# An mLSTM cell with mixture-of-depths: where gates, stores, weights and expert layers stand in a hand-ordered schedule

## The chip, the core and the metric

The kernel runs on one core of a Trainium2 chip. A core has TensorE (PE; its weight loads are shown as PEld), VectorE (DVE), ScalarE (ACT), GpSimd (POOL) and SyncE (SP), which take their instructions each from a queue of its own, in the order in which the program puts them there, and wait for one another at semaphores. SyncE issues nearly all transfers, which 16 DMA engines carry out; GpSimd issues the indirect ones. The metric is the time of one execution on the device in microseconds, lower is better. Beside it stands the span from the first to the last instruction, which the profile divides up.

## The reference

Four batches, eight heads, 768 positions, heads of 40. First a recurrent cell with a matrix state for each head, then a feed-forward network for the 128 rows of each batch that score highest:

```python
for t in range(S):
    m_new = np.maximum(f_gate[:, :, t] + m, i_gate[:, :, t])
    f_stab, i_stab = np.exp(f_gate[:, :, t] + m - m_new), np.exp(i_gate[:, :, t] - m_new)
    C = f_stab[..., None, None] * C + i_stab[..., None, None] * np.einsum('bhd,bhe->bhde', vt, kt)
    n = f_stab[:, :, None] * n + i_stab[:, :, None] * kt
    h_tilde = np.einsum('bhde,bhe->bhd', C, qt)
    denom = np.maximum(np.abs(np.einsum('bhd,bhd->bh', n, qt))[:, :, None], 1.0)
    y[:, :, t] = 1.0 / (1.0 + np.exp(-o_gate[:, :, t])) * h_tilde / denom
# x: y with the heads side by side, (4, 768, 320)
scores = np.einsum('bsd,d->bs', x, w_gate)
for b in range(B):
    top_idx = np.argpartition(-scores[b], capacity)[:capacity]       # capacity 128
    xe = x[b, top_idx]
    ye = np.maximum(xe @ w1, 0.0) @ w2                                # 320 -> 1024 -> 320
    out[b, top_idx] = xe + sigmoid(scores[b, top_idx])[:, None] * ye  # other rows: x
```

All is float32. The inputs and the output are in device memory.

## The kernel before

`_fast` computes the cell in chunks: 12 steps, n = 0 to 11, of 256 positions each, three to a batch (batch b = n // 3). All stabilising factors are worked out once at the start from the two gate arrays (`gate_rows`, `gate_cols`); the result is a column of factors for each step.

**One step.** TensorE runs `scores(n)` (k times q, line 307), then for the next step `turn(n+1, "kT")` (the transposes of k, line 241, with `fill` matmuls of line 230 ahead of them in some steps) and `update(n+1)` (v times k, line 274), then `read(n)` (state times q, 329), `turn(n+1, "qT")` and `attend(n)` (masked scores times v, 339). VectorE masks the scores (`masked`, 313), sums the states (`states`, 286 to 294) and divides (`divide`, 348 to 353) into a tile y. ScalarE copies the transposes out of PSUM (243, 245), widens q (225) and takes the sigmoid of the output gate (`sigmoid`, 257). GpSimd multiplies v by its factors two steps ahead (`weigh(n+2)`, 253) and y by the gate (`output`, 361, two instructions), which gives x, the rows of the bridge between both parts.

**Buffers.** k, q and v have three each, the gate o four, y four, x two (batches alternate). A load into a buffer waits for the last reader of what it held.

**Loads.** `load(n)` puts v, k (two transfers each) and q (one) of step n on SyncE, and in most steps the gate of step n-1 (four transfers). It is called three steps ahead. `store(n)` writes x of a step to the output in two transfers; `load` holds some of these, and others stand in the loop. The weights of the expert (eight transfers) are put on SyncE in step 5. SyncE also holds a transfer until the eighth before it has landed.

**The expert of a batch.** `router(n)` (376) takes a step's scores on VectorE. `spread(b)` (404, 408) brings the 768 scores of a batch into every partition, `ranks(b)` counts for each score how many are greater, three columns on VectorE (414) and three on ScalarE (419), `select(b)` (453) makes a one-hot tile `sel` of it, `numbers(b)` (498, 459 to 464) the row numbers, `fetch(b)` (504) brings these rows back out of the output by an indirect transfer on GpSimd; it waits for the batch's stores. `fetched(b)` (514 to 518) transposes them, `layer1` (543 to 549, two calls for two halves) and `layer2` (559) are the network, `weighed` (564) applies the gate of the expert, and `add(b)` (568) adds the result into the output by an indirect transfer. The last batch, 3, is done in another way: its rows are picked out of x by matmuls (`picked`, 479), and its scores are spread in two parts (`ranks_first`, `ranks_last`).

**Where the expert's parts stand before.** Batch 0: `spread` in step 3, `ranks` and `select` in step 5, `numbers` at the end of step 5, `fetch` at the end of step 6 ahead of which `weigh(8)` and behind which `weigh(9)` stands on GpSimd, layers in step 8. Batch 1: `spread` in step 6, `numbers` and `fetch` in step 8, `layer1` in step 9, `layer2` in step 10. Batch 2: `spread` in step 9, `ranks` in step 10 directly behind `layer2(1)`, `fetch` in step 10, the first half of `layer1` in step 11 and the second half behind the loop. TensorE's order in the loop is written out by hand; no scheduler moves anything. What follows the loop from `router_last` on is the end of batch 3 with `layer2(2)` in it.

Of the kernel before, what the change touches and what calls it, by code (L numbers as in the profile page):

```python
# [9 lines left out]
FP = mybir.dt.float32  # L10
# [16 lines left out]
def _fast(ctx, tc, q, k, v, i_gate, f_gate, o_gate, w_gate, w1_in, w2_in, out):  # L27
# [32 lines left out]
    def load_kv(n, t, src):  # L60
        b, s = divmod(n, NS)
        for c in range(2):
            a = s * 256 + c * 128
            SP.dma_start(out=t[n % NB][:, c, :, 0:D], in_=src[b, :, a:a + 128, :].rearrange("h p d -> p h d"))
# [12 lines left out]

    def load(n):

        if n < N:  # L80
            load_kv(n, v_t, v)
            load_kv(n, k_t, k)
            for i in {8: (2,), 9: (3, 4, 5)}.get(n, ()):
                store(i)
            load_q(n)
            for i in {7: (0, 1)}.get(n, ()):
                store(i)
        for i in {7: (), 8: (), 9: (6, 7, 8), 11: (), 12: (10, 11)}.get(n, (n - 1,) if n <= N else ()):
            load_o(i)

    for t, src in ((f_sb, f_gate), (i_sb, i_gate)):
# [21 lines left out]
    load_kv(2, v_t, v)  # L113
    load_kv(2, k_t, k)
    load_q(2)
    load_o(1)
    ident = const.tile([128, 128], FP, name="ident")

    def zero(t):
# [223 lines left out]
    def divide(n):  # L343
        b, s = divmod(n, NS)
        pH = pending[n]["pH"].rearrange("s h r x -> s r h x")
        den = work.tile([128, 2, H], FP, name="den")
        nq = pH[:, :, :, D]
        DVE.scalar_tensor_tensor(out=den, in0=nq, scalar=-1.0, in1=cols[s][:, 2:4, b * H:b * H + H], op0=OP.mult, op1=OP.max)
        DVE.scalar_tensor_tensor(out=den, in0=nq, scalar=LEAST * LEAST, in1=den, op0=OP.max, op1=OP.max)
        rec = work.tile([128, 2, H], FP, name="rec")  # L350
        DVE.reciprocal(out=rec, in_=den)
        y = work.tile([128, 2, H, D], FP, name="y", bufs=4)
        DVE.tensor_tensor(out=y, in0=pH[:, :, :, 0:D], in1=rec.unsqueeze(3).to_broadcast([128, 2, H, D]), op=OP.mult)
        pending[n]["y"] = y

# [231 lines left out]
    zero(wv_t[2].rearrange("s c h r x -> s c h (r x)"))  # L587
    zero(k_t[2][:, :, :, D:DP])
    weigh(1)
    for n in range(N):  # L590
        b, s = divmod(n, NS)
        more = n + 1 < N
        late = b > 1 and s == 1
        given = late or n == 5
        if n > 0:
            load(n + 3)
        if n == 5:
            for h in range(2):
                f, g = slice(512 * h, 512 * h + 512), slice(2 * h, 2 * h + 2)
                SP.dma_start(out=w1[:, :, f], in_=w1_in[0:256, f].rearrange("(j p) f -> p j f", j=2))  # L600
                for i in range(2):
                    SP.dma_start(out=w1c[64 * i:64 * i + 64, g],
                                 in_=w1_in[256:DM, :].rearrange("p (f i e) -> p i f e", i=2, e=128)[:, i, g])
            for h in range(2):
                SP.dma_start(out=w2[:, 4 * h:4 * h + 4], in_=w2_in[512 * h:512 * h + 512].rearrange("(f p) d -> p f d", p=128))
        for i in {10: (9,), 11: (10,)}.get(n, ()):
            store(i)
        scores(n)
        masked(n)
        if n == 8:  # L610
            fetched(0)
            numbers(1, ps_t.tile([128, 3], FP, name="pi", tag="t"))
            fetch(1)
        if n == 8:
            valued(0)
        if n == 0:
            update(0)
            load(3)
            states(0)
        if n == 8:  # L620
            layer1(0, 0)
            layer1(0, 4)
            layer2(0, 0, 4)
            layer2(0, 4)
        if n == 10:
            layer2(1)
        if given:
            ranks(b - 1)
            select(b - 1)
        if n in (8, 10):  # L630
            weighed(n // 2 - 4)
        if n == 9:
            fetched(1)
            sigmoid(8)
            output(8)
            for i in range(6, 9):
                store(i)
            weigh(10)
            layer1(1, 0)
            layer1(1, 4)  # L640
            valued(1)
            router(6)
            router(7)
        early = n in (3, 6) or n > 8
        if n > 0 and early:
            router(n - 1)
        if more:
            turn(n + 1, "kT", (0, 2, 2, 2, 2, 3, 4, 5)[n] if n < 8 else 0)
            widen(n + 1)
        if 0 < n and more:  # L650
            update(n + 1)
            states(n + 1)
        if 0 < n < 7 and not early:
            router(n - 1)
        if not more:
            sigmoid(n)
            gated(n)
            fill(ps_t.tile([128, 128], FP, name="pf", tag="t"), 2)
        read(n)
        if n == 10:  # L660
            numbers(b - 1, spare(n + 1)[:, 1, 0:3])
        if n + 2 < N and n != 8:
            weigh(n + 2)
        if n == 10:
            fetch(2)
        if n == 0:
            update(1)
            states(1)
        if more:
            turn(n + 1, "qT")  # L670
            if b > 0 and s == 0:
                dep[b - 1] = {"sb": spread(b - 1, 0, 2 * NS)}
            if n not in (6, 7, 8):
                sigmoid(n)
        else:
            fetched(b - 1, 2)
            dep[b] = {"sb4": spread(b, 0, 4)}
            layer1(b - 1, 0)
            valued(b - 1)
            ranks_first(b)  # L680
        attend(n)
        divide(n)
        if n == 5:
            numbers(b - 1, spare(n + 1)[:, 1, 0:3])
        if n == 8:
            for i in (6, 7):
                sigmoid(i)
                output(i)
        elif more and n not in (6, 7):
            output(n)  # L690
        if n == 6:
            fetch(0)
        if n in (8, 10):
            add(n // 2 - 4)
        if n == 0:
            tables()
        if n == 1:
            margins()
    b = B - 1
    router_last(N - 1)  # L700
    output(N - 1)
    layer1(b - 1, 4)
# [371 lines left out]
```

## Time and profile before

| | |
|---|---|
| median of 14 runs | 169.01 us (167.5 to 171.79) |
| the profiled execution | 168.81 us |
| its span | 167.1 us |
| PE busy | 147.9 us, 88% |
| PEld, DVE, ACT, POOL busy | 128.7, 94.7, 75.9, 68.9 us |
| DMA queue of SyncE and its packets | 93472, 22.36 MB, 71.7% of 16 engines' span |
| granted TensorE clock, mean | 0.978 |

The times of TensorE's parts, from its timeline: the scores of steps 1 to 11 start at 20.32, 28.35, 36.81, 45.57, 53.94, 62.72, 72.12, 81.15, 99.56, 118.40 and 130.22 us; the layers of batch 0 run from 82.24 to 92.91; `layer2(2)` starts at 141.66, the last matmul of `layer2(3)` ends at 159.95, and the rest of the span is the last indirect add.

In lines of a timeline the columns are start, length, engine, source line, operation, out<-in, shapes and count, and in brackets the idle time ahead of it and what ended it. In lines of waits they are engine and line, what it waited for, us in total, how often, and the longest. Packets of 160 bytes (k, v and o, whose rows are 40 floats) make up 73728 of the trace's 94438, with a mean of 16.3 ns each.

### The profile page before, as it was taken

The numbers are of one execution on the slowest core, as the hardware profiler recorded it, in microseconds if no ns is written. First come the engines' busy times: TensorE is split into PE (matmuls) and PEld (weight loads), VectorE is DVE, ScalarE is ACT, GpSimd is POOL, SyncE is SP. The second block draws the span as 40 slices with busy tenths as digits, with TensorE's granted clock in tenths as the row PEclk, the third lists the DMA queues.
The fourth block names the chain that finished last, engine by engine and source line by source line (L and its number), as shares of the span: only waits on it lengthen the run. The fifth ranks groups of instructions, "written<-read, shape, count | busy, mean of one in ns | idle before, by whom it ended". The sixth has DMA issues, their size and how long they took to land.

```text
span 167.1 us, 6707 instructions
## 1 busy us (share of the span) xinstructions
PE 147.9 (88%) x2872; PEld 128.7 (77%) x2872; DVE 94.7 (57%) x250; ACT 75.9 (45%) x144; POOL 68.9 (41%) x89
## 2 busy tenths in 40 slices
PE   7999989799989797997999996949999999999920
PEld 7888879697969696996897785739869989799710
DVE  6576456476655999869620049633695796802000
ACT  1576564443626952494421353441935339521110
POOL 7045293909082907262006128953410682230030
PEclk9999999999999999999999999986999999999995
DMA  4999989898899979789968988999687160330003
GB/s 88 194 161 162 177 150 152 138 155 162 146 188 153 172 133 254 131 196 319 323 143 179 231 154 127 167 191 178 115 184 205 47 118 4 80 36 4 8 12 43
DMA packets 94424, 24.14 MB, mean 145 GB/s; under 512 B 88465, under 2 KB 93778, under 8 KB 94386
## 3 DMA queue, kind: packets, MB, share of 16 engines
q1 hardware_dynamic: 93472, 22.36, 71.7%
q0 software_dynamic: 720, 1.15, 4.2%
q8 instruction: 24, 0.39, 1.0%
q10 hardware_dynamic: 194, 0.13, 0.3%
q14 instruction: 14, 0.11, 0.2%
HBM read 19.04 MB, written 4.59 MB: 141 GB/s over the span
## 4 chain that ended last, share of the span: by engine, by line
PE 48%; DMA 14%; DVE 11%; SPq 8%; POOL 7%; issue 6%; ACT 2%; POOLq 1%; DVEq 0%
PE pt L241 7%; PE pH L339 6%; PE pU L274 6%; DMA v<-in_v_dram 5%; PE py L559 5%; PE pU L543 5%; POOL wv L253 4%; SPq L75 4%; PE pH L329 4%; DMA q<-in_q_dram 3%; PE warm L107 3%; DMA out_dram<-yg,idx 3%; SPq L368 3%; PE pS L307 3%; POOL x L361 2%
## 5 line engine op out<-in xcount | busy, mean ns | idle before, releaser
L253 POOL TENSOR_TENSOR wv<-v,cols 64x656 f32<-64x656 f32 x23 | 30.9, 1343 | 49.8 <-DMA v<-in_v_dram 42.4
L361 POOL TENSOR_TENSOR x<-y,o 128x320 f32<-128x320 f32 x24 | 21.5, 931 | 12.1 <-ACT o L257 4.1
L245 ACT COPY qT<-pt 128x512 f32<-128x512 f32 x24 | 13.8, 634 | 18.9 <-PE pt L241 18.9
L243 ACT COPY kT<-pt 128x512 f32<-128x512 f32 x24 | 13.5, 586 | 17.1 <-PE pt L241 16.9
L274 PE MATMUL pU<-wv,k 128*64 128x82 f32 x384 | 17.3, 244 | 3.1 <-POOL wv L253 2.0
L286 DVE TENSOR_TENSOR C<-pU,C 128x164 f32<-128x164 f32 x40 | 13.1, 328 | 10.8 <-PE pU L274 9.7
L274 PEld LDWEIGHTS pU<-wv,k 128*64 128x64 f32 x384 | 15.2, 142 | 5.2 <-POOL wv L253 3.9
L376 DVE CUSTOM_DVE_ANT_0 scr<-x,wg 128x320 f32<-128x320 f32 x22 | 16.2, 734 | 4.6 <-POOL x L361 2.7
L559 PE MATMUL py<-w,hT 128*128 128x320 f32 x64 | 18.2, 437 | 0.0
L241 PE MATMUL pt<-ident,k 128*128 128x128 f32 x96 | 14.1, 278 | 3.7 <-DMA k<-in_k_dram 3.2
L339 PE MATMUL pH<-wv,P 128*64 128x82 f32 x384 | 16.3, 237 | 0.0
L339 PEld LDWEIGHTS pH<-wv,P 128*64 128x64 f32 x384 | 14.4, 136 | 2.0 <-issue 1.5
L241 PEld LDWEIGHTS pt<-ident,k 128*128 128x128 f32 x96 | 10.6, 141 | 6.2 <-PE pt L241 3.8
L559 PEld LDWEIGHTS py<-w,hT 128*128 128x128 f32 x64 | 11.8, 190 | 4.7
L313 DVE TENSOR_TENSOR P<-pS,mask 128x1024 f32<-128x1024 f32 x12 | 14.6, 1214 | 0.9 <-PE pS L307 0.9
L307 PE MATMUL pS<-qT,kT 40*64 40x64 f32 x768 | 14.3, 221 | 0.8 <-issue 0.4
L329 PE MATMUL pH<-C,qT 40*64 40x41 f32 x704 | 14.6, 234 | 0.0
L241 PE MATMUL pt<-ident,qw 128*128 128x128 f32 x96 | 13.1, 279 | 1.4 <-ACT qw L225 1.4
L329 PEld LDWEIGHTS pH<-C,qT 40*64 40x64 f32 x704 | 13.2, 140 | 1.3 <-issue 0.5
L307 PEld LDWEIGHTS pS<-qT,kT 40*64 40x64 f32 x768 | 12.5, 134 | 2.1 <-issue 0.6
L568 POOL DMA_INDIRECT out_dram<-yg,idx x4 | 6.5, 1620 | 16.6 <-ACT yg L564 16.3
L419 ACT ACTIVATE sgn<-sb,x 128x768 f32<-128x768 f32 (+2 forms) x16 | 12.8, 800 | 0.4
(138 smaller groups left out, 213.3 us busy)
## 6 DMA issues: line engine op xcount, KB each, us to landing
k<-in_k_dram SPq DMA_DIRECT2D x24, 160.0 KB, 4.6
q<-in_q_dram SPq DMA_DIRECT2D x12, 320.0 KB, 5.7
v<-in_v_dram SPq DMA_DIRECT2D x24, 160.0 KB, 4.3
o<-in_o_gate_dram SPq DMA_DIRECT2D x48, 80.0 KB, 3.9
out_dram<-x SPq DMA_DIRECT2D x24, 160.0 KB, 2.7
w<-in_moe_w_dram SPq DMA_DIRECT2D x2, 640.0 KB, 8.3
w<-in_moe_w_dram SPq DMA_DIRECT2D x2, 512.0 KB, 6.5
w1c<-in_moe_w_dram SPq DMA_DIRECT2D x4, 64.0 KB, 5.6
```

Source lines behind the costliest of these rows:

```text
L241: PE.transpose(pt[:, p, :], src[:, c, 2 * p:2 * p + 2, :].rearrange("s j d -> s (j d)"), ident)
L243: ACT.copy(out=T[:, :, 128 * c:128 * c + 128], in_=pt)
L245: ACT.copy(out=T.rearrange("e p (u t) -> e t p u", t=2)[:, c], in_=pt)
L253: (DVE if n == 0 and r else POOL).tensor_tensor(out=wv_t[n % 3][o, :, :, r], in0=v_t[n % NB][o], op=OP.mult, in1=cols[s][o, 0:2, b * H:b * ...
L274: PE.matmul(pU[64 * j:64 * j + 64, c, p], k_t[n % NB][:, c, 2 * p + j, :], wv_t[n % 3][:, c, 2 * p + j], start=True, stop=True)
L307: PE.matmul(pS[o, j, c, p, :], kT[e, p, t], qT[e, p, t], start=True, stop=True)
L313: DVE.tensor_tensor(out=P.rearrange(flat), in0=pending[n].pop("pS").rearrange(flat), op=OP.mult, in1=mask.unsqueeze(1).to_broadcast([128, ...
L329: PE.matmul(g["pH"][64 * c:64 * c + 64, NP * j + p, r], g["qT"][e, p, t], state[n, 2 * c + r][e, p, :], start=(c, j) not in g["begun"], st ...
L339: PE.matmul(g["pH"][64 * c:64 * c + 64, NP * j + p], g["P"][:, j, c, p, :], wv_t[n % 3][:, c, 2 * p + j], start=(c, j) not in g["begun"], ...
L361: POOL.tensor_tensor(out=x.rearrange(order, j=2, d=D), in0=pending[n]["y"][:, r].rearrange("s (j p) d -> s j p d", j=2), in1=o.rearrange(o ...
L376: DVE.tensor_tensor_reduce(out=scr, in0=x[:, r, 0:DM], in1=wg, scale=1.0, scalar=0.0, op0=OP.mult, op1=OP.add, accum_out=x[:, r, DM:DM + 1])
L559: PE.matmul(d["py"], d["hT"][:, f, :], w2[:, f, :], start=(f == 0), stop=(f == NF - 1))
```

## The change

The order of many calls changes; no instruction of the mathematics does. `load` brings v, k and q alone, and a gate only where a small table says so: gate 0 with step 3's load, gate 1 with step 5's, gate 2 with step 6's, gates 3, 4 and 5 with step 10's. Gates 6 to 9 come in step 10, gates 10 and 11 in step 11. The y tiles have eight buffers. A new `opened(n)` is the sigmoid and the `output` of a step; it stands up to seven steps behind the step's `divide`. The three stores of batch 0 and the weights stand in step 6 behind `load(8)` and ahead of `load(9)`, which moves into the middle of that step. Ranks, numbers and fetch of batch 0 stand in step 7, those of batch 1 in step 10, its layers in step 11; ranks of batch 2 in step 11, and its numbers, fetch and the whole of its network behind the loop. Fills in `turn` remain in steps 5, 6 and 10 only.

```diff
     def load(n):
-        if n < N:
-            load_kv(n, v_t, v)
-            load_kv(n, k_t, k)
-            for i in {8: (2,), 9: (3, 4, 5)}.get(n, ()):
-                store(i)
-            load_q(n)
-            for i in {7: (0, 1)}.get(n, ()):
-                store(i)
-        for i in {7: (), 8: (), 9: (6, 7, 8), 11: (), 12: (10, 11)}.get(n, (n - 1,) if n <= N else ()):
+        load_kv(n, v_t, v)
+        load_kv(n, k_t, k)
+        load_q(n)
+        for i in {3: (0,), 5: (1,), 6: (2,), 10: (3, 4, 5)}.get(n, ()):
             load_o(i)
...
-    load_o(1)
...
-        y = work.tile([128, 2, H, D], FP, name="y", bufs=4)
+        y = work.tile([128, 2, H, D], FP, name="y", bufs=8)
...
+    def opened(n):
+        sigmoid(n)
+        output(n)
...
+        if 0 < n < 9 and n != 6:
             load(n + 3)
         scores(n)
         masked(n)
+        if n == 6:
+            opened(2)
+            for i in range(3):
+                store(i)
+            weights()
+            load(9)
...
+        if n == 7:
+            ranks(0)
+            select(0)
         if n == 8:
             fetched(0)
             valued(0)
             layer1(0, 0)
             layer1(0, 4)
-            layer2(0, 0, 4)
-            layer2(0, 4)
+            layer2(0)
+            weighed(0)
+        if n == 9:
+            weigh(10)
         if n == 10:
+            opened(5)
+            for i in range(3, 6):
+                store(i)
+            for i in range(6, 10):
+                load_o(i)
+            router(3)
+            router(4)
+        if n in (4, 6):
+            router(n // 2 - 2)
+        if n == 6:
+            router(2)
         if more:
-            turn(n + 1, "kT", (0, 2, 2, 2, 2, 3, 4, 5)[n] if n < 8 else 0)
+            turn(n + 1, "kT", {5: 2, 6: 2, 10: 6}.get(n, 0))
             widen(n + 1)
         if 0 < n and more:
+            if n == 10:
+                router(5)
+                dep[1] = {"sb": spread(1, 0, 2 * NS)}
             update(n + 1)
             states(n + 1)
+            if n == 10:
+                ranks(1)
+                select(1)
         if not more:
+            fetched(1)
+            layer1(1, 0)
+            valued(1)
+            opened(6)
+            opened(7)
+            opened(8)
+            layer1(1, 4)
+            for i in range(6, 9):
+                router(i)
+                store(i)
+            load_o(10)
+            load_o(11)
+            layer2(1)
+            weighed(1)
+            opened(9)
+            dep[2] = {"sb": spread(2, 0, 2 * NS)}
+            ranks(2)
+            select(2)
         read(n)
         if n + 2 < N and n != 8:
             weigh(n + 2)
...
         if more:
             turn(n + 1, "qT")
+        if n == 6:
+            dep[0] = {"sb": spread(0, 0, 2 * NS)}
+        if n in (7, 10):
+            numbers(n // 3 - 2, spare(n + 1)[:, 1, 0:3])
+            fetch(n // 3 - 2)
         attend(n)
         divide(n)
+        if n in (3, 5):
+            opened(n // 2 - 1)
+        if n == 9:
+            opened(3)
+            opened(4)
         if n == 8:
+            add(0)
...
     b = B - 1
+    numbers(2, ps_t.tile([128, 3], FP, name="pi", tag="t"))
+    router(9)
+    opened(10)
+    fetch(2)
+    router(10)
+    store(9)
+    store(10)
+    sigmoid(N - 1)
+    gated(N - 1)
+    add(1)
+    dep[b] = {"sb4": spread(b, 0, 4)}
+    fetched(2, 2)
+    layer1(2, 0)
+    valued(2)
+    ranks_first(b)
     router_last(N - 1)
```

`weights()` holds the eight transfers that stood in step 5's branch. The calls that these lines replace in the loop, the routers, sigmoids, outputs, stores and expert parts of before, are gone from there.

More of the change, by code (lines that the diff above doesn't have):

```diff
@@ L589, in _fast, with weights @@
     weigh(1)
+    def opened(n):
+        sigmoid(n)
+        output(n)
+    def weights():
+        for h in range(2):
+            f, g = slice(512 * h, 512 * h + 512), slice(2 * h, 2 * h + 2)
+            SP.dma_start(out=w1[:, :, f], in_=w1_in[0:256, f].rearrange("(j p) f -> p j f", j=2))
+            for i in range(2):
+                SP.dma_start(out=w1c[64 * i:64 * i + 64, g],
+                             in_=w1_in[256:DM, :].rearrange("p (f i e) -> p i f e", i=2, e=128)[:, i, g])
+        for h in range(2):
+            SP.dma_start(out=w2[:, 4 * h:4 * h + 4], in_=w2_in[512 * h:512 * h + 512].rearrange("(f p) d -> p f d", p=128))
     for n in range(N):
@@ L592, in _fast @@
         more = n + 1 < N
-        late = b > 1 and s == 1
-        given = late or n == 5
-        if n > 0:
+        if 0 < n < 9 and n != 6:
             load(n + 3)
[L597 to L607, printed above, removed]
         scores(n)
         masked(n)
[L610 to L615, printed above, removed]
+        if n == 6:
[4 more added lines that the diff above has]
+            load(9)
         if n == 0:
@@ L619, in _fast @@
             states(0)
+        if n == 7:
+            ranks(0)
+            select(0)
         if n == 8:
+            fetched(0)
+            valued(0)
             layer1(0, 0)
             layer1(0, 4)
-            layer2(0, 0, 4)
-            layer2(0, 4)
+            layer2(0)
+            weighed(0)
+        if n == 9:
+            weigh(10)
         if n == 10:
[L626 to L636, printed above, removed]
-                store(i)
[L638 to L646, printed above, removed]
+            opened(5)
+            for i in range(3, 6):
+                store(i)
+            for i in range(6, 10):
+                load_o(i)
@@ L647, in _fast @@
+            router(3)
[4 more added lines that the diff above has]
+            router(2)
         if more:
-            turn(n + 1, "kT", (0, 2, 2, 2, 2, 3, 4, 5)[n] if n < 8 else 0)
+            turn(n + 1, "kT", {5: 2, 6: 2, 10: 6}.get(n, 0))
             widen(n + 1)
         if 0 < n and more:
+            if n == 10:
+                router(5)
+                dep[1] = {"sb": spread(1, 0, 2 * NS)}
             update(n + 1)
             states(n + 1)
-        if 0 < n < 7 and not early:
-            router(n - 1)
+            if n == 10:
+                ranks(1)
+                select(1)
@@ L655, in _fast @@
         if not more:
-            sigmoid(n)
-            gated(n)
-            fill(ps_t.tile([128, 128], FP, name="pf", tag="t"), 2)
+            fetched(1)
[13 more added lines that the diff above has]
+            opened(9)
@@ L659, in _fast @@
+            dep[2] = {"sb": spread(2, 0, 2 * NS)}
+            ranks(2)
+            select(2)
         read(n)
-        if n == 10:
-            numbers(b - 1, spare(n + 1)[:, 1, 0:3])
         if n + 2 < N and n != 8:
             weigh(n + 2)
-        if n == 10:
-            fetch(2)
         if n == 0:
@@ L670, in _fast @@
             turn(n + 1, "qT")
[L671 to L680, printed above, removed]
+        if n == 6:
[3 more added lines that the diff above has]
+            fetch(n // 3 - 2)
         attend(n)
         divide(n)
-        if n == 5:
-            numbers(b - 1, spare(n + 1)[:, 1, 0:3])
-        if n == 8:
[L686 to L694, printed above, removed]
+        if n in (3, 5):
[3 more added lines that the diff above has]
+            opened(4)
+        if n == 8:
+            add(0)
         if n == 0:
```

## The prediction

> **What bounds the kernel now.** I read the page's slices first, then the waits, then TensorE's, GpSimd's and SyncE's timelines around step 8, then the stretches of one table by stage. The slices:
>
> ```profile
> PE   7999989799989797997999996949999999999920
> ...
> PEclk9999999999999999999999999986999999999995
> DMA  4999989898899979789968988999687160330003
> ```
>
> TensorE and the DMA engines are both near full over the first three fifths; behind that the DMA engines fall idle and TensorE alone is full. In stages (columns: length, then busy time of PE, PEld, DVE, ACT, POOL, then clock, DMA share, GB/s):
>
> ```profile
> 21.90:81.15 59.25, 54.44 (x1422) 48.49 (x1422) 41.70 (x105) 31.32 (x55) 29.63 (x42) 1.00 0.90 177
> 99.60:111.50 11.90, 8.20 (x125) 6.87 (x123) 8.71 (x19) 4.59 (x11) 9.97 (x9) 1.00 0.92 157
> 111.50:115.50 4.00, 3.96 (x81) 3.74 (x82) 1.63 (x5) 0.73 (x1) 0.15 (x1) 0.57 1.16 175
> 138.80:159.90 21.10, 21.10 (x147) 17.49 (x145) 7.83 (x32) 7.84 (x23) 3.44 (x3) 1.00 0.15 26
> ```
>
> To be seen: TensorE idles only 4.8 us in steps 2 to 7, and nothing in the last stage, where every transfer, rank and pick that batch 2 needs has been made ready under other matmuls. The third line is a stretch at a half clock behind a thin one. The longest waits:
>
> ```profile
> POOL wv L253 <- DMA v<-in_v_dram: 42.4, 9, 11.7
> POOL xe L504 <- DMA out_dram<-x: 12.5, 2, 8.0
> ```
>
> GpSimd waits for v with nothing lost so far, since little stands behind it in its queue. What does stand around the longest of these waits is the point on which I build:
>
> ```profile
> 71.39 2.65 POOL L253 TENSOR_TENSOR wv<-v,cols 64x656 f32<-64x656 f32 x2 [3.33 <-DMA v<-in_v_dram]
> 75.39 1.25 POOL L504 DMA_INDIRECT xe<-out_dram,idx  x1 [1.36 <-DVE P L313]
> 88.34 2.64 POOL L253 TENSOR_TENSOR wv<-v,cols 64x656 f32<-64x656 f32 x2 [11.71 <-DMA v<-in_v_dram]
> ...
> 72.94 0.67 SPq L600 DMA_DIRECT2D w<-in_moe_w_dram  x1
> ...
> 79.47 4.22 SPq L64 DMA_DIRECT2D v<-in_v_dram  x2
> ...
> 82.24 0.55 PE L514 MATMUL pX<-ident,xe 128*128 128x128 f32 x3
> ```
>
> The fetch of batch 0's rows goes out at 75.39, ahead of `weigh(9)`, which waits for v of step 9 until 88.34 because the weights went first. TensorE takes the fetched rows at 82.24.
>
> **Steps 0 to 8.** Removed ahead of step 8's scores: 16 of the 20 fills of `turn`, at 0.272 us (ten records took 1.36 us), 4.35 us; and TensorE's waits for k, wv and qw, 0.99, 0.38, 0.54, 0.85, 0.97 and 1.01 us, 4.74 us, as the gates of steps 3 to 5 no longer stand before k and v. Added: `numbers(0)` now follows `ranks(0)` and `select(0)` in one step. On VectorE these are the mask 1.13, three comparisons of 1.06 from start to start, 0.20 and 0.88, 5.4 us after the scores; TensorE has turn 1.02, update 1.28, read 1.07 and turn 1.02 for it, 4.4: a wait of 1.0. Scores of step 8: 81.15 - 4.35 - 4.74 + 1.0 = 73.1, done at 74.2. Eight us are won.
>
> **The fetch of batch 0.** They are lost at once. `fetch(0)` now stands behind `weigh(9)` on GpSimd, and v of step 9 stands on SyncE behind three stores and all weights. When does it land? Against before, only the gates of steps 3 to 5 have left the queue ahead of it: 12 transfers of 512 packets, at 16.3 ns a packet (mean of the 160-byte packets in the trace) over 16 engines 0.52 us each, 6.2 us. With the engines at 0.90 they set the pace, so 88.3 - 6.2 = 82.1. Were it the queue's position alone, the weights would start at about 62 (step 6 at 57 by the sums above, its mask, `output(2)` at 1.69, the stores at 0.63 an issue) and v would land 15.4 us later, as from 72.94 to 88.34: 77.5. I take 82.1, nearest to a full engine, and keep 77.5. Then two multiplications 2.65, and the indirect transfer, 4.7 us from issue to landing (median; 3.0 to 6.2): TensorE has the rows at 89.5 instead of 82.24, after idling 15 us. Behind it wait both layers, step 8's update and all else on TensorE; the gain in steps 0 to 7 costs or saves nothing beyond this point. The layers of batch 0: 82.24 to 92.91 without the 0.3 of `numbers(1)`, 10.4, to 99.9. The half clock (below) adds 1.7: 101.6. The rest of step 8 took 6.65, of which 0.63 were waits for yg and qw: 6.0, to 107.6. Step 9, now without layers: scores 1.09, turn 1.02, update 1.28, read 0.80, turn 1.02, attend 1.29, with gaps 6.6: 114.2.
>
> **Step 10.** Scores 1.09, six fills 1.63, turn 1.02: 117.9. `spread(1)` needs `router(5)`, that `output(5)`, the third in a row on GpSimd at 1.69 each behind the sigmoid of step 3, which follows step 9's qT copies on ScalarE: 114.0 + 5.1 + 0.7 = 119.8. TensorE waits 1.5 with the transposes; spread ends at 119.9. Then `ranks(1)` waits for step 11's states, 2.4 after spread; three comparisons 3.2, 0.2 and 0.9: `numbers(1)` at 126.6, 3.3 later than update, read and turn (3.4) would let it. In the kernel before this ranking ran under the 4.4 us of `layer2(1)` and cost nothing; that cover is gone. End of `numbers(1)` 126.9, attend to 128.2, step 11's scores to 129.3.
>
> **Step 11.** The index takes 0.6, the fetch 4.7: rows at 132.2, a wait of 2.9. Two layers 10.4, and 1.7 for the clock: 144.3. `output` of steps 6 to 8 (5.1 us of GpSimd from about 137, behind the fetch and three sigmoids of 0.74) hides under the layers. `spread(2)` 0.66: 145.0. `ranks(2)`: copy 0.80, 3.2, 0.2, 0.9, thus 150.1, with read and attend (2.4) as the only cover: a wait of 2.7. `numbers(2)` to 150.4.
>
> **The end.** `fetch(2)` stands behind `output(10)` on GpSimd, whose gate is queued behind the stores of step 8: output of step 8 at 142.5, two stores and four loads at 0.63, landing 3.9, sigmoid 0.74, output 1.69: 152.1. Rows 4.7 later, 156.8; TensorE has some 1.0 us of work meanwhile. Transposes and copies 1.2, first half of the layer 2.63, a buffer that waits for its relu 0.8, second half 2.63, spread 0.37: `layer2(2)` at 164.4. From there all is as it was: in the timeline 141.66 to the span's end at 167.1, 25.4. That gives 189.8, and 1.7 for the clock, 191.5 of span. The profiled execution took 168.81 with a span of 167.1, and lies 0.2 below the median, so 1.9 are added: 193.4 us. Eight y buffers in place of four cost no instruction; they let the multiplication wait.
>
> **The clock.** In 108.40 to 111.90 TensorE was busy 1.36 of 3.5 us, no single gap above 1.45, and the next 3.40 us ran at 0.50: half of it, 1.7, is the price. I charge it behind the 15 us gap, step 11's fetch (3.3 and 2.9 idle close together) and the gap before `fetched(2)`; none to two more are the bounds.
>
> The Trainium skill, TensorE: Matmul & The Clock Gate, "HAM oscillation — how this bites in real kernels", lets only gaps above some 3.4 us throttle the clock; by it I would charge two, and the sum would be 191.7, an estimate. It also speaks against the change, which opens such gaps. The skill's DMA: Bandwidth & Descriptors, "Anatomy of one DMA — SWDGE (gpsimd) path", gives 2.0 us plus bytes over 436 GB/s, 2.4 us for the 164 KB of a fetch, where the row has 4.7; three fetches by that rule would give 186.5, an estimate again.
>
> **Rivals.** *v in time.* SyncE keeps so far ahead that v of step 9 lands before `numbers(0)` is done. For it: step 8 comes 8 us sooner and the queue is shorter. Against: a DMA share of 0.90 over the whole stretch. Then fetch(0) goes at about 74 and lands at 78.7: 10.8 us less, 182.6 us. *Late gates.* The gates of steps 6 to 9 are 16 transfers behind three stores in step 10; if their queue drains at the 7.11 us that eight of them took before, output 6 starts some 4 us later, and the same happens to gates 10 and 11 before `fetch(2)`: 8 us more, 201 us. For it: POOL and SyncE carry all of this in order. Against: the DMA share is below 0.66 there. *No gain in front.* If k and v came no earlier, since their three buffers are freed by TensorE, the sum stays: v of step 9 sets it. *All covered* ends on the other side: the fetch for batch 0 is not held up by `weigh(9)` and every wait of steps 10 and 11 hides, so that only the 8 us in front and the old 1.7 of the clock remain: 169.0 - 9.7 = 159.3. It decides once the new waits of `spread(1)`, `numbers(1)`, `fetched(1)`, `numbers(2)` and `fetched(2)` (1.5, 3.3, 2.9, 2.7 and 5.4 by the sums above, 15.8) come below 9.7 together and the 15 us gap is closed. Against it stands that each has its cover counted out above.
>
> **How the numbers follow.** My forecast holds 0.68, late gates 0.15, v in time 0.13, all covered 0.04. The time is the forecast's, 193.4. Its bounds: v at 77.5 (-4.6), clock charges from none (-5.1) to five (+3.4), three fetches at 3.0 or 6.2 each (-5.1, +4.5). They do not all fall one way; I let the range run from 184 to 203, which takes in late gates and most of the way to v in time. A measurement of this kernel tells changes of 0.5% from none; for faster by more than that 0.03 remain, for within it 0.01, for slower 0.96.
>
> **What would show it.** In the profile of the changed kernel: scores of step 8 near 73; GpSimd's longest wait for v right before a fetch, with TensorE idle some 10 to 15 us before the transposes of xe; three more waits of 2 to 5 us on TensorE for `sel` and xe after 115; half clock behind them; the last layer2 of batch 2 to the end unchanged at 25 us. I am wrong if the fetch of batch 0 lands before TensorE asks for it, or if the ranks of steps 10 and 11 end under matmuls.

## The result, and the profile after

| | before | after |
|---|---|---|
| median | 168.96 us (166.14 to 174.77, 47 runs) | 199.04 us (195.69 to 203.16, 10 runs) |
| the profiled execution | 168.81 us | 204.79 us |
| its span | 167.1 us | 202.5 us |
| PE busy | 147.9 us | 157.0 us |
| granted TensorE clock, mean | 0.978 | 0.882 |

The change makes the kernel slower, by a ratio of 1.1771, 95% interval [1.1703, 1.184]. Executions of one kernel differ by up to some 5%, the longer ones mostly at a lower granted clock; medians take them all, ratios only those within 1.5% of the shortest. The profiled execution lies 2.9% above the median, so lengths of stages read from it are good to a few us only. The slices of the changed kernel:

```profile
PE   7998899899999768008999986675996149899940
...
PEclk9999999999999996755999997875799655999996
DMA  5999888867899999998983027672036652202003
```

Where TensorE had two thin slices (6 and 4, between 100 and 113 us) there are now four thin places (from 66, 81, 122 and 152 us on), and a stretch at a lower clock in or behind each of them. The stages show how much is lost in each (length; busy time of PE, PEld, DVE, ACT, POOL; clock, DMA share, GB/s):

```profile
79.00:92.70 13.70, 2.38 (x69) 1.82 (x67) 3.11 (x7) 0.42 (x2) 3.81 (x3) 0.62 1.06 184
92.70:104.30 11.60, 11.59 (x64) 9.70 (x65) 0.00 (x0) 1.76 (x5) 0.00 (x0) 0.82 1.03 147
117.20:138.40 21.20, 13.63 (x299) 11.46 (x297) 15.05 (x38) 8.09 (x15) 6.84 (x7) 0.83 0.61 118
...
151.70:176.30 24.60, 14.83 (x170) 11.72 (x169) 12.86 (x39) 11.32 (x24) 10.55 (x11) 0.72 0.52 104
176.30:194.50 18.20, 18.20 (x121) 14.88 (x119) 4.20 (x19) 5.52 (x17) 1.59 (x1) 1.00 0.09 12
```

TensorE stands idle for 11.3 of the first 13.7 us, for 7.6 of the stretch from 117.20 and 9.8 of the one from 151.70. The last stretch is the end of the last batch, full and at full clock as it was. In the list of waits (us in total, times, longest) the same places carry names:

```profile
POOL wv L247 <- DMA v<-in_v_dram: 31.0, 5, 15.4
...
PE pX L508 <- DMA xe<-out_dram,idx: 14.4, 3, 10.9
...
PEld L492 <- DVE sel L447: 8.1, 3, 3.4
```

GpSimd waits for v less than before in total (31.0 for 42.4), but TensorE now waits for fetched rows three times and for a one-hot tile three times. The timelines of GpSimd, SyncE and TensorE around them:

```profile
83.36 2.62 POOL L247 TENSOR_TENSOR wv<-v,cols 64x656 f32<-64x656 f32 x2 [15.37 <-DMA v<-in_v_dram]
86.28 1.25 POOL L498 DMA_INDIRECT xe<-out_dram,idx  x1 [0.29 <-POOL wv L247]
...
74.62 2.77 SPq L64 DMA_DIRECT2D v<-in_v_dram  x2
...
76.36 0.30 PE L492 MATMUL pU<-place,sel 128*128 128x3 bf16 x6 [2.35 <-DVE C L280]
91.37 0.87 PE L508 MATMUL pX<-ident,xe 128*128 128x128 f32 x3 [10.87 <-DMA xe<-out_dram,idx]
92.71 3.78 PE L537 MATMUL pU<-xeT,w 128*128 128x128 f32 x16 [0.46 <-ACT xeT L510]
...
133.04 0.31 PE L492 MATMUL pU<-place,sel 128*128 128x3 bf16 x6 [3.18 <-DVE sel L447]
138.39 0.88 PE L508 MATMUL pX<-ident,xe 128*128 128x128 f32 x3 [1.77 <-DMA xe<-out_dram,idx]
158.72 0.32 PE L492 MATMUL pi<-place,sel 128*128 128x3 bf16 x6 [2.91 <-DVE sel L447]
166.93 0.90 PE L508 MATMUL pX<-ident,xe 128*128 128x128 f32 x3 [1.75 <-DMA xe<-out_dram,idx]
```

Batch 0's row numbers were complete at 77.24 (its index on VectorE). The fetch that needs them went out at 86.28, directly behind the multiplication of v, whose transfer was issued only at 74.62. Nine us passed in which everything that the fetch needs was there.

By stages of the two profiles the difference of the spans, 35.4 us, divides as follows. Up to the scores of step 8: 2.2 won (81.15 to 78.97). From there to step 9's scores 13.0 lost, from 18.4 to 31.4. Steps 9 and 10: 30.7 to 24.2, but 10.4 of layers moved out, so 4.0 lost. From step 11's scores to `layer2(2)`: 11.4 to 41.7, of which 10.4 are the layers that moved in, so 19.8 lost. The rest 25.4 to 26.2.

### The profile page after: what moved, and what is told of

It reads as the page before. It is cut to its first block, busy times and chain, and to the rows that moved or that the text cites. A ratio compares the mean times of both kernels' runs of the same rounds, so it can differ in the third digit from the quotient of the medians.

```text
span 202.5 us, 6676 instructions
## 1 busy us (share of the span) xinstructions
PE 157.0 (78%) x2848; PEld 134.4 (66%) x2848; DVE 97.6 (48%) x250; ACT 75.5 (37%) x144; POOL 71.1 (35%) x89
## 4 chain that ended last, share of the span: by engine, by line
PE 42%; issue 14%; DMA 12%; DVE 10%; POOL 8%; SPq 6%; ACT 3%; ACTq 1%; POOLq 0%; DVEq 0%
PE pt L235 6%; PE pH L333 6%; PE pU L537 6%; DVE scr L370 5%; PE pU L268 5%; DMA xe<-out_dram,idx 4%; PE py L553 4%; PE pS L301 4%; SPq L75 4%; POOL x L355 4%; DMA k<-in_k_dram 4%; PE pH L323 3%; POOL wv L247 3%; DMA o<-in_o_gate_dram 2%; PE ph L537 2%
## 5 line engine op out<-in xcount | busy, mean ns | idle before, releaser
L355 POOL TENSOR_TENSOR x<-y,o 128x320 f32<-128x320 f32 x24 | 23.5, 1030 | 24.7 <-ACT o L251 11.9
L370 DVE CUSTOM_DVE_ANT_0 scr<-x,wg 128x320 f32<-128x320 f32 x22 | 18.3, 830 | 11.2 <-POOL x L355 8.8
L239 ACT COPY qT<-pt 128x512 f32<-128x512 f32 x24 | 13.7, 631 | 17.5 <-PE pt L235 17.5
L301 PE MATMUL pS<-qT,kT 40*64 40x64 f32 x768 | 16.0, 233 | 2.1 <-issue 1.8
L333 PE MATMUL pH<-wv,P 128*64 128x82 f32 x384 | 17.5, 246 | 0.0
L537 PE MATMUL pU<-xeT,w 128*128 128x128 f32 x80 | 15.3, 370 | 2.1 <-ACT xeT L510 1.4
L537 PEld LDWEIGHTS pU<-xeT,w 128*128 128x128 f32 x80 | 14.2, 275 | 3.6 <-ACT xeT L510 2.7
L301 PEld LDWEIGHTS pS<-qT,kT 40*64 40x64 f32 x768 | 13.9, 145 | 3.9 <-issue 2.5
L333 PEld LDWEIGHTS pH<-wv,P 128*64 128x64 f32 x384 | 15.4, 144 | 1.5 <-issue 1.0
L508 PE MATMUL pX<-ident,xe 128*128 128x128 f32 (+1 forms) x9 | 2.6, 432 | 14.4 <-DMA xe<-out_dram,idx 14.4
L235 PE MATMUL pt<-ident,k 128*128 128x128 f32 x96 | 13.3, 278 | 0.3 <-ACT yg L558 0.2
```

The costliest lines, as they stand in the source:

```text
L235: PE.transpose(pt[:, p, :], src[:, c, 2 * p:2 * p + 2, :].rearrange("s j d -> s (j d)"), ident)
L239: ACT.copy(out=T.rearrange("e p (u t) -> e t p u", t=2)[:, c], in_=pt)
L301: PE.matmul(pS[o, j, c, p, :], kT[e, p, t], qT[e, p, t], start=True, stop=True)
L333: PE.matmul(g["pH"][64 * c:64 * c + 64, NP * j + p], g["P"][:, j, c, p, :], wv_t[n % 3][:, c, 2 * p + j], start=(c, j) not in g["begun"], ...
L355: POOL.tensor_tensor(out=x.rearrange(order, j=2, d=D), in0=pending[n]["y"][:, r].rearrange("s (j p) d -> s j p d", j=2), in1=o.rearrange(o ...
L370: DVE.tensor_tensor_reduce(out=scr, in0=x[:, r, 0:DM], in1=wg, scale=1.0, scalar=0.0, op0=OP.mult, op1=OP.add, accum_out=x[:, r, DM:DM + 1])
```

## The experiments

All of them compute what the two kernels compute. What their texts call the prediction's account (theory A) is the one on record above: the held fetch, then rankings without cover, then the half clock. The rival that each sets against it is told in each.

**The fetch ahead of the multiplication.** Step 7's `weigh(9)` moves behind `fetch(0)`:

```diff
-        if n + 2 < N and n != 8:
+        if n + 2 < N and n not in (7, 8):
             weigh(n + 2)
...
             fetch(n // 3 - 2)
+        if n == 7:
+            weigh(9)
```

> The changed kernel with one pair swapped: in step 7 weigh(9) stands behind fetch(0) on GpSimd instead of ahead of it. Theory A (the fetch is held up by weigh(9), which waits for v of step 9): the index was ready at 77.2 us and the fetch went at 86.3, so the rows come some 9 us sooner, scores of step 9 start near 100 instead of 110.4, and the time falls by 9 to 11 us to about 189. Rival B (the rows or the weights are late themselves: stores of batch 0 or the weights land only about 86): the fetch or layer1 waits for those instead and the time falls by less than 3 us. Rival C (the half clock after gaps is the larger part): the gap shrinks to 2 to 4 us, some clock comes back too, and the fall is above 12 us.

Measured: 191.13 us (190.27 to 193.67), ratio 1.1202 [1.1108, 1.1297]. Its timelines of GpSimd and TensorE:

```profile
79.31 1.26 POOL L498 DMA_INDIRECT xe<-out_dram,idx  x1 [10.82 <-DVE den L342]
84.41 2.78 POOL L247 TENSOR_TENSOR wv<-v,cols 64x656 f32<-64x656 f32 x2 [3.85 <-DMA v<-in_v_dram]
...
84.95 0.87 PE L508 MATMUL pX<-ident,xe 128*128 128x128 f32 x3 [4.80 <-DMA xe<-out_dram,idx]
103.44 1.16 PE L301 MATMUL pS<-qT,kT 40*64 40x64 f32 x64
```

The two instructions have changed places, v comes a us later than in the changed kernel, and step 9's scores start at 103.44 instead of 110.41. So the place in GpSimd's queue costs the changed kernel 7.0 us in this stage and 8 us of medians, which sets aside both rivals, under 3 and above 12. It is less than the 9 to 11 expected: the fetch left 7.0 us sooner and not 9, and the rows came 6.4 sooner. The wait of 4.80 that remains is the transfer itself, which the kernel before had hidden too.

**The load ahead of the weights.** Step 6 puts v, k and q of step 9 on SyncE before the weights:

```diff
-            weights()
             load(9)
+            weights()
```

> The changed kernel with load(9) put on SyncE ahead of the eight weight transfers (behind the stores). The order on GpSimd stays. Theory A: v of step 9 is issued some 5.3 us sooner (69.3 instead of 74.6), weigh(9) and the fetch follow by 5 to 9 us sooner, and the time falls by 5 to 10 us, to 189 to 194, less than or as much as with the swap on GpSimd; the weights come 4 to 6 us later and still before the layers. Rival B (weights or stores bound the layers): the layers wait for the weights and the time stays within 2 us of 199.

Measured: 196.23 us (192.81 to 197.11) beside 170.43 of the kernel before, 3 us below the changed kernel's median where 5 to 10 were expected. Its timelines:

```profile
76.35 2.68 POOL L247 TENSOR_TENSOR wv<-v,cols 64x656 f32<-64x656 f32 x2 [7.15 <-DMA v<-in_v_dram]
79.39 1.25 POOL L498 DMA_INDIRECT xe<-out_dram,idx  x1 [0.36 <-POOL wv L247]
...
85.08 0.87 PE L508 MATMUL pX<-ident,xe 128*128 128x128 f32 x3 [3.39 <-DMA xe<-out_dram,idx]
```

v came 7 us sooner and the fetch goes out as early as in the run before. The layers then did not wait for the weights, so that rival falls, and the weights queued ahead of v are confirmed as what made `weigh(9)` late. From step 8's scores to step 9's this profile takes 24.25 us and that of the run before 24.45, where the changed kernel takes 31.44: in the stage that both repair, the two moves are worth the same. The span is 3 us longer than in the run before (194.3 for 191.3), of which 1.2 are there before step 8's scores and 2.1 come between the rows of batch 1 and those of batch 2, in parts that neither edit touches. Why they are there is open; the times of the two runs overlap.

**The same move in the kernel before.** `fetch(0)` goes from the end of step 6 to behind `weigh(9)` in step 7, nothing else:

```diff
-        if n == 6:
-            fetch(0)
...
             weigh(n + 2)
+        if n == 7:
+            fetch(0)
```

> The kernel before with one call moved: fetch(0) stands behind weigh(9) in step 7 instead of ahead of it in step 6. Nothing else of the change is in it. Theory A (one held-up fetch by itself costs this much): weigh(9) waits for v until 88.3 in the kernel before, so the fetch goes out near 91 instead of 75.4, the rows come near 96 instead of 81, TensorE stands 13 to 14 us, and the time rises by 11 to 16 us, to 180 to 185 (with some half clock). Rival (a late fetch is hidden by what TensorE does otherwise, and it is the moved layers and ranks that cost): the time rises by less than 4 us.

Measured: 181.67 us (180.48 to 182.6), ratio 1.0622 [1.0506, 1.0738], 10.2 us, a little under what was expected. Its timelines:

```profile
90.03 2.62 POOL L253 TENSOR_TENSOR wv<-v,cols 64x656 f32<-64x656 f32 x2 [13.35 <-DMA v<-in_v_dram]
92.95 1.25 POOL L504 DMA_INDIRECT xe<-out_dram,idx  x1 [0.29 <-POOL wv L253]
...
97.58 0.87 PE L514 MATMUL pX<-ident,xe 128*128 128x128 f32 x3 [12.92 <-DMA xe<-out_dram,idx]
```

The rows come 15.3 us later than in the kernel before (82.24) and the span grows by 13.4. Three instructions exchanged in one queue, without any other part of the change, make the first thin place.

**Batch 1's layers late, in the kernel before.** `fetched(1)`, `layer1(1)`, `layer2(1)` and `weighed(1)` go from steps 9 and 10 to the start of step 11, `add(1)` behind the loop:

```diff
-        if n == 10:
-            layer2(1)
...
         if n == 9:
-            fetched(1)
...
-            layer1(1, 0)
-            layer1(1, 4)
-            valued(1)
...
         if not more:
+            fetched(1)
+            layer1(1, 0)
+            layer1(1, 4)
+            valued(1)
+            layer2(1)
+            weighed(1)
```

> The kernel before with one part of the change alone: the transposes, both layers and the weighing of batch 1 stand at the beginning of step 11 (they stood in steps 9 and 10), its add behind the loop. Matmuls, ranks, gates and fetches are as before. Theory D: the layers no longer cover the landing of step 10's k and v in step 9 (TensorE would wait some 5 us there) nor ranks(2) in step 10 (some 4 to 5 us ahead of numbers(2)); the time rises by 7 to 11 us, to 176 to 181. Rival F (a moved matmul costs nothing, as TensorE is full anyway): within 2 us of 169.

Measured: 182.28 us (181.06 to 182.72), with the kernel before at 169.71 (166.5 to 172.09) beside it: 12.6 us of medians, more than expected. TensorE's timeline shows what the layers had covered, and below it the same places in the kernel before:

```profile
106.86 2.17 PE L241 MATMUL pt<-ident,k 128*128 128x128 f32 x8 [5.65 <-DMA k<-in_k_dram]
111.62 2.46 PE L274 MATMUL pU<-wv,k 128*64 128x82 f32 x32 [2.60 <-POOL wv L253]
...
127.58 0.30 PE L498 MATMUL pU<-place,sel 128*128 128x3 bf16 x6 [4.43 <-DVE C L286]
```

```profile
108.11 0.66 PE L241 MATMUL pt<-ident,k 128*128 128x128 f32 x4 [0.26 <-DMA k<-in_k_dram]
109.46 0.63 PE L241 MATMUL pt<-ident,k 128*128 128x128 f32 x4 [0.69 <-DMA k<-in_k_dram]
111.53 2.16 PE L274 MATMUL pU<-wv,k 128*64 128x82 f32 x32 [1.45 <-POOL wv L253]
```

5.65 and 2.60 are the landing of step 10's k and v, most of which the layers had covered while the queue drained; 4.43 is a wait for VectorE, which ranks batch 2 just there. Together they are 12.7, and 2.4 of the first two were there in the kernel before. So 10.3 of the 12.2 us by which the span grew (167.1 to 179.3) are waits that the layers had lain over. The rest is not told apart; 17.1 us of this span ran at half clock up to the last matmul, where the kernel before had 3.4, and the transposes behind the first wait took 2.17 where eight take 1.09 at full clock.

**Both in the kernel before.**

> The kernel before, with both edits that were tried in it singly: fetch(0) behind weigh(9) in step 7 (by itself 1.0622 of the time before) and batch 1's layers at the start of step 11 (by itself 12.6 us). If the two costs are separate they add up: some 23 us, a ratio of 1.13 to 1.14 and about 193 us. If the second gap hides behind the first, or the late fetch of batch 0 only delays work that step 11 then waits for anyway, the sum is smaller, 14 to 17 us. What the changed kernel costs beyond this (1.177) belongs to the late gates, ranks and numbers of steps 10 and 11.

Measured: 193.95 us (192.35 to 195.63), ratio 1.1468 [1.1316, 1.1619], with the kernel before at 168.62. TensorE's timeline:

```profile
95.49 0.88 PE L514 MATMUL pX<-ident,xe 128*128 128x128 f32 x3 [12.50 <-DMA xe<-out_dram,idx]
...
123.94 2.45 PE L274 MATMUL pU<-wv,k 128*64 128x82 f32 x32 [7.31 <-POOL wv L253]
...
139.68 0.30 PE L498 MATMUL pU<-place,sel 128*128 128x3 bf16 x6 [4.42 <-DVE C L286]
```

The costs add up: 25.3 us of median. The three waits are 24.2 together, where the kernel before waited 2.4 for step 10's k and v, and the span is 24.0 longer than before (191.1). Two moves by themselves thus cost most of the 30 us that the change costs. The changed kernel lies 0.030 of the time before above this one, some 5 us, with the intervals of both ratios apart; by its repetition below (1.1683) it is 0.022, and there the intervals overlap.

**Cover for the rankings.** The first experiment's kernel, with gates 6 to 8 loaded ahead of stores 3 to 5 and opened in step 10, stores 6 to 8 and gates 10 and 11 ahead of batch 1's layers, and batch 2's ranking put under `layer2(1)`:

```diff
         if n == 10:
+            for i in range(6, 9):
+                load_o(i)
...
         if not more:
+            for i in range(6, 9):
+                store(i)
+            load_o(10)
+            load_o(11)
             fetched(1)
...
             for i in range(6, 9):
                 router(i)
-                store(i)
-            load_o(10)
-            load_o(11)
+            dep[2] = {"sb": spread(2, 0, 2 * NS)}
+            ranks(2)
+            select(2)
             layer2(1)
             weighed(1)
             opened(9)
...
+            numbers(2, ps_t.tile([128, 3], FP, name="pi", tag="t"))
+            fetch(2)
...
+        if n == 10:
+            opened(6)
+            opened(7)
+            opened(8)
```

> The first experiment's kernel (weigh(9) behind fetch(0)) with batch 2's ranking put under matmuls again: gates 6 to 8 are loaded ahead of the stores of steps 3 to 5, output 6 to 8 stand in step 10 behind fetch(1), and in step 11 the routers, spread(2), ranks(2) and select(2) stand ahead of layer2(1), numbers(2) and fetch(2) behind it. The matmuls are the same. Theory D (what is left over after the swap are rankings and fetches of steps 10, 11 and behind the loop with no matmuls over them): numbers(2) waits 1 us instead of 2.9, the wait for the rows of batch 2 goes, and the time falls by 3 to 5 us against the first experiment, to 186 to 188. Rival E (the half clock and VectorE's slow routers set the end): within 1.5 us of 191.

Measured: 188.51 us (186.9 to 189.62), with the kernel before at 169.71: 2.6 less than the fetch's move alone, a little under the 3 to 5 expected, the runs of the two not overlapping. In TensorE's timeline:

```profile
142.75 0.31 PE L492 MATMUL pi<-place,sel 128*128 128x3 bf16 x6 [1.02 <-DVE sel L447]
```

`numbers(2)` waits 1.02 where it waits 2.90 in the first experiment's kernel, and the rows of batch 2, for which TensorE waits 1.06 there, are in time; the wait for step 9's router behind the loop grows to 3.58 from 2.14. The ranking can be covered, and part of the wait in step 11 was it; the remaining 19 us of loss are not in this place.

**The last fetch ahead of `output(10)`.**

```diff
     numbers(2, ps_t.tile([128, 3], FP, name="pi", tag="t"))
+    fetch(2)
     router(9)
     opened(10)
-    fetch(2)
```

> The changed kernel with fetch(2) directly behind numbers(2), ahead of router(9) and output(10). If output(10) in front of it holds the fetch up, as the prediction has it, the fetch is issued at about 160.6 instead of 162.95, the rows reach TensorE 2.4 us sooner, and the time falls by 2 to 2.5 us. If the row transfer waits for the stores or the end waits for router(10), which then comes 1 us later, the time stays within 1 us.

Measured: 200.81 us (198.75 to 206.44), ratio 1.1804 [1.1673, 1.1935]: no gain, the second of the two answers. Its timelines of GpSimd, VectorE and TensorE:

```profile
158.25 1.12 POOL L498 DMA_INDIRECT xe<-out_dram,idx  x1 [6.01 <-DMA o<-in_o_gate_dram]
...
160.30 2.76 DVE L370 CUSTOM_DVE_ANT_0 scr<-x,wg 128x320 f32<-128x320 f32 x1 [1.21 <-POOL x L355]
...
163.12 0.47 PE L398 MATMUL pB<-ident,x 128*128 128x128 f32 x1 [3.50 <-DVE x L370]
164.89 0.85 PE L508 MATMUL pX<-ident,xe 128*128 128x128 f32 x3
```

The fetch left 1.8 us behind the end of `numbers(2)` instead of 3.9. But TensorE now waits 3.50 for step 10's router in front of the rows, whose one instruction took 2.76 us while GpSimd multiplied, and takes the rows 8.75 behind the start of `numbers(2)` as against 8.2. At this place two waits end within a us or two of each other, and to shorten one uncovers the other.

**The clock.** Four kernels put dummy matmuls (`fill`) into the gaps. In the changed kernel: into all of them (first), and in front of the three networks, with 46 and with 38 in the first gap (third and fourth); in the first experiment's kernel into all of them (second). The third's edit:

```diff
-            fetched(0)
+            fetched(0, 46)
...
-            fetched(1)
+            fetched(1, 5)
...
-    fetched(2, 2)
+    fetched(2, 4)
```

> The changed kernel with dummy matmuls (fill) put where TensorE waits: 6 ahead of numbers(0), 36 ahead of the transposes of fetched(0), 9 ahead of numbers(1), 5 ahead of fetched(1), 8 ahead of numbers(2), 6 ahead of the last spread and 4 more ahead of fetched(2). No wait is removed. Theory A with the clock as a second cause: 44 us ran at half clock; with the gaps filled the granted clock stays near 1.0 (mean above 0.95 instead of 0.88) and the time falls by 6 to 10 us, to 189 to 193. Rival (most of the half clock lies under waits and costs little): the clock returns but the time falls by less than 3 us.

> The swap of the first experiment and the fills of the third together (5 fills instead of 36 ahead of fetched(0), as the gap there is short). If the held-up fetch and the clock are two causes that add: the time falls by 15 to 19 us, to 180 to 184; what is left over 169 are the waits of steps 10 and 11 and behind the loop. If they are one cause seen twice (the clock falls only because of the one long gap), the fall is that of the first alone, 9 to 12.

> The changed kernel with fills only directly ahead of the three expert networks that stood at half clock: 46 ahead of fetched(0), 5 ahead of fetched(1), 4 instead of 2 ahead of fetched(2), sized to end before the rows land. Theory A (the half clock is a cost of its own, 2.5, 2.8 and 2.2 us in these three stretches): the time falls by 4 to 8 us against the changed kernel. Rival (what the clock takes there is given back by the waits that follow, or fills bring none of it, as the earlier fills did): within 2 us of the changed kernel.

> As the fills directly ahead of the three networks, but 38 instead of 46 ahead of fetched(0), since 46 ended 3 us after the rows had landed. Theory A (the half clock costs some 6.7 us in the three networks, and the fills of the run before gave part of it back by holding the transposes): the time falls by 4 to 7 us against the changed kernel's 199 to 201. Rival: within 2.5 us of it again.

Measured beside a repetition of the changed kernel itself,

> The changed kernel unchanged, on the same chip as the next one, so that the two can be compared: 199 us, between 196 and 202.

which gave 200.96 us (196.83 to 204.95) and a ratio of 1.1683 [1.1576, 1.179]: all gaps 200.38 us, 1.1802 [1.1711, 1.1892]; fetch first and all gaps 197.53 us (192.3 to 199.53), in none of its runs below the shortest of the fetch's move alone (190.27); 46 fills 198.61 us, 1.1636 [1.1524, 1.1748]; 38 fills 197.89 us, 1.1712 [1.1626, 1.1797]. TensorE's timeline with 46, then with 38:

```profile
81.32 12.41 PE L224 MATMUL pX<-hot 128*128 128x128 f32 x92
94.20 0.55 PE L508 MATMUL pX<-ident,xe 128*128 128x128 f32 x3 [0.47 <-DMA xe<-out_dram,idx]
95.21 2.05 PE L537 MATMUL pU<-xeT,w 128*128 128x128 f32 x16 [0.46 <-ACT xeT L510]
```

```profile
76.45 8.75 PE L224 MATMUL pX<-hot 128*128 128x128 f32 x76
89.60 0.71 PE L508 MATMUL pX<-ident,xe 128*128 128x128 f32 x3 [4.40 <-DMA xe<-out_dram,idx]
90.78 3.23 PE L537 MATMUL pU<-xeT,w 128*128 128x128 f32 x16 [0.46 <-ACT xeT L510]
```

With 46 the first sixteen matmuls of the layer take 2.05 us instead of 3.78 in the changed kernel, and the three networks 10.67, 10.6 and 7.64 instead of 12.94, 13.27 and 9.38: 6.7 us shorter. But the rows came at 94.20 instead of 91.37, since the fetch was issued 1.6 us later in this profile (87.90) and took longer, and the time moved by 2.4 us of medians with overlapping intervals. The fills themselves ended at 93.73, ahead of the rows, and not 3 us behind them as the last expectation has it. With 38 the fills ended at 85.2, 4.4 us were left, and the layer's first matmuls took 3.23. The mean clock rose from 0.882 to between 0.92 and 0.95, and no measurable time came of it: the gains expected of all four runs stayed out.

## Why the prediction was right or wrong

*Direction and account: right; the size too low.* 193.4 us were forecast and 199.04 measured, with the bounds 184 and 203. The time alone lies nearer to the rival *Late gates* with its 201 us, so what speaks for the forecast are the places: the losses are where it named them, and two of them were made alone in the kernel before. In spans 191.5 were forecast and the profile, of an execution 2.9% above the median, has 202.5, 11.0 more: 1.9 at the rows of batch 0, 0.9 in its layers and the rest of step 8, 3.6 in steps 9 and 10, 5.5 from step 11's scores to `layer2(2)` and 0.8 behind it, less the third charge for the clock, 1.7, which the forecast adds at the end.

*The front: eight us won, the term that was mis-sized most.* 2.2 came, and step 8's scores started at 78.97 instead of 73.1. This did not enter the time, since the forecast has the gain lost at the fetch, but it made the wait there 10.87 us instead of 15. From the scores of step 1 to those of step 6 TensorE takes 37.5 us instead of 42.4, 4.9 less. Then step 6 takes 10.0 for 9.4 and step 7 10.5 for 9.0, and step 1 itself starts 0.6 later. In step 6 the spread waits 1.17 for the router of step 2; the kernel before had six transposes of a spread in this step too, batch 1's, without a wait. In step 7 `numbers(0)` waits 2.35, not 1.0: by the profile for the states (C), which stand in VectorE's queue behind three rankings and the one-hot tile, and which the sum had not counted there:

```profile
74.39 0.96 DVE L447 TENSOR_TENSOR sel<-iota,cnt 128x768 bf16<-128x768 f32 x1
75.26 1.05 DVE L280 TENSOR_TENSOR C<-pU,C 128x164 f32<-128x164 f32 x3
```

One of the six waits that the sum takes out, 0.97, is in its row no wait for k, wv or qw but one for VectorE, which finished the row numbers; it went with them. A ranking that moves into a step delays what VectorE does for that same step.

*The fetch behind `weigh(9)`: right in place, in time partly by luck.* v at 83.36 for 82.1, rows at 91.37 for 89.5; the 1.9 is less than the spread between the two ends that were kept. But 82.1 supposes that the DMA engines set the pace, and the other end, by position in the queue, had the weights start at 62; they started at 69.33. With that start the position gives 84.7, as near to 83.36 as 82.1 is, so the two ways are not told apart. That v's lateness comes of its place on SyncE behind the weights is shown by moving it. The cost, with 8 us taken back by the one exchange, is shown too. *v in time* and *all covered* fall with it.

*The layers of batch 0* were put at 10.4 + 1.7 and took 12.94. *Steps 9 and 10*: 20.6 from step 9's scores to step 11's forecast (107.6 to 128.2), measured 24.2. The routers were missing: their instructions took 0.92 us each under GpSimd's multiplications and not 0.49, `spread(1)` ended 8.1 behind step 10's scores instead of 5.7, and the update behind it ran at the half clock in 2.44. Here `numbers(1)` waits 3.18 for `sel`, 3.3 in the forecast. *Step 11 and the end*: from step 11's scores to `layer2(2)` the forecast has 36.2 (128.2 to 164.4), measured 41.7. The waits came where they were put: 1.77 for the rows (2.9 forecast), 2.91 for `sel` (2.7), and 8.2 from the start of `numbers(2)` to the rows (6.7). Of the surplus 2.9 are in the two networks at a half clock, 1.3 between batch 1's layers and `numbers(2)`, where the last routers and transposes follow one another with gaps, and 1.5 from `numbers(2)` to the rows. The forecast's own terms for that last place give 152.6 and not 152.1 for `output(10)`. The last part, 25.4 forecast, took 26.2.

*Late gates*: there in part. ScalarE's timeline:

```profile
144.71 0.60 ACT L543 ACTIVATE hT<-pU 128x512 f32<-128x512 f32 x1 [4.60 <-PE pU L541]
145.29 1.98 ACT L251 ACTIVATE o<-o 128x640 f32<-128x640 f32 x3
...
159.76 0.74 ACT L251 ACTIVATE o<-o 128x640 f32<-128x640 f32 x1 [2.29 <-DMA o<-in_o_gate_dram]
```

`output(6)` ran at 146.11 instead of about 137, but its gate was not what it waited for: its sigmoid follows the relu of batch 1's layer on ScalarE without a wait. `output(10)` ran at 160.57, where the prediction had it at 150.4, and its gate landed only shortly before (ScalarE waits for it until 159.76). Of the ten us 6.4 were already there at step 11's scores, and the row numbers were not complete before 160.55 either. But to take `fetch(2)` out from behind it brought nothing, so the claim that this order alone sets the end is not borne out.

*The clock: mechanism right, size open.* 5.1 us were charged, for three stretches. Up to TensorE's last matmul one of 3.4 us ran at half clock before, and five with 44.4 us in the changed kernel's profile; the networks were 6.7 us longer there than with 46 fills. The rule on gaps that the prediction cites beside its charge does not fit here: only one of TensorE's gaps, the 10.87, is above 3.4 us, and the next is 3.18. Yet filling the gaps brought no more than 0 to 2.4 us. In the profile of the third kernel the rows came 2.8 us later, which hides part of what the clock gave; with fills in all gaps and with 38 they came at 90.17 and 89.60, so it does not go with fills as such. What the half clock costs apart from the waits is not settled.

*What stays open.* Some 4 to 5 us of the loss come neither of the fetch nor of the layers moved in the kernel before. What is left over for them are the gates, routers and rankings of steps 6 to 11 and the clock behind them, which no run moved one by one in the kernel before; covering the ranking gave back 2.6, and nothing was found that gives back the rest. Why the second experiment's times lie above the first's, with the same gain in the stage that both repair, stays open as well.

## What to carry to other kernels

Before you move an instruction, look at what it then stands behind in its own queue and when *that* is released: a multiplication that waits for a late transfer held a ready fetch for 9 us here, and exchanging them was worth 8. Dense work between two waits is a cover with a price: moving batch 1's layers away cost 12.6 us, and 10.3 us of new waits stand where they had lain. And where several waits end close together, expect one repair to uncover the next, as the last fetch did, and check it before counting its gain.

## What the hardware showed beyond this

The router's multiply-and-add on VectorE is one instruction for 128x320 values. The source view gives its min, median and max in ns, for the kernel before and then for the changed one:

```profile
L376 DVE CUSTOM_DVE_ANT_0 scr<-x,wg x22: 481/493/2378, 26.0 to 134.2; 128x320 f32<-128x320 f32 x22
```

```profile
L370 DVE CUSTOM_DVE_ANT_0 scr<-x,wg x22: 480/916/1343, 46.3 to 163.3; 128x320 f32<-128x320 f32 x22
```

The median doubles although instruction and operands are the same. In the changed kernel's VectorE timeline the last of three that start inside GpSimd's multiplications (these end at 123.22) is long, as the two ahead of it are, and the next is short:

```profile
122.66 0.91 DVE L370 CUSTOM_DVE_ANT_0 scr<-x,wg 128x320 f32<-128x320 f32 x1
123.72 0.49 DVE L370 CUSTOM_DVE_ANT_0 scr<-x,wg 128x320 f32<-128x320 f32 x1
```

The Trainium skill, SBUF — State Buffer, "SBUF: two separate sides", states that VectorE and GpSimd share one pair of ports, and that a VectorE instruction with two inputs from SBUF and a GpSimd one that reads SBUF exclude each other: the first holds the pair for its whole instruction. These rows agree: 0.42 us of 0.91 are beyond the 0.49 that it takes alone, and in the run with the last fetch moved 2.3 of 2.76, while GpSimd multiplied until 0.36 us before its end.

The clock stood at one half in stretches of 3.41, 10.24 and 13.65 us within the changed kernel, one, three and four times the 3.41 of the single stretch in the kernel before. An indirect fetch of 128 rows took 3.4 to 6.3 us from the start of its issue to TensorE's first use of the rows wherever TensorE waited for it: 133.96 to 137.33 in the run with fills in all gaps is the shortest, 87.90 to 94.20 in the run with 46 fills the longest. The 2.4 us that the prediction worked out as an estimate from DMA: Bandwidth & Descriptors of the Trainium skill is not met by any of them.
